# A decode kernel over a 65,536-row cache: V's loads moved from SP's DMA queue to ACT's

## The chip, the core and the metric

The kernel runs on one core of a Trainium2 chip, as one program. The core has a matrix engine (TensorE, PE), a vector engine (VectorE, DVE), a scalar engine (ScalarE, ACT), GpSimd (POOL) and SyncE (SP), each with its own program, and 16 DMA engines that all of them can give transfers to. A transfer is put on the queue of the engine that issues it. The engines wait for each other and for transfers through semaphores that the program names. The metric is the time of one execution on the device in microseconds (us); smaller is better. The median before the change is 2522.78 us over three runs (2522.70 to 2523.16).

## The reference

One token is decoded by an attention block and by a gated MLP, and the two are mixed by a gate:

```python
q = (x @ wq).reshape(B, Sq, H, Dh).transpose(0, 2, 1, 3)          # 1 x 32 x 1 x 128
scores = jnp.einsum("bhqd,bhkd->bhqk", q, k_cache) * (Dh ** -0.5) # k_cache: 1 x 32 x 65536 x 128, bf16
p = softmax(scores, axis=-1)
o = jnp.einsum("bhqk,bhkd->bhqd", p, v_cache)                     # v_cache: as k_cache
a = o.transpose(0, 2, 1, 3).reshape(B, Sq, H * Dh) @ wo
b = (silu(x @ w_gate) * (x @ w_up)) @ w_down                      # 512 -> 1792 -> 512
g = sigmoid((x * gate_w).sum(-1, keepdims=True))
out = g * a + (1 - g) * b
```

The two caches are 32 heads x 65,536 rows x 128 bf16 each, 537 MB each. Each byte is needed once, for one query.

## The kernel before

**Pieces and places.** A head's K and its V are each loaded in two halves of 8.39 MB: 128 partitions with 64 KB each (256 cache rows of 256 bytes), by one DMA. I call them K(h,0), K(h,1), V(h,0) and V(h,1). All lie in one SBUF tensor, `mem`, addressed in KB of a partition (`at(kb, n)`, L107). K(h,0) is at KA = 32 to 96 and K(h,1) at KZ = 0 to 64, so the two overlap in 32 to 64. V(h,0) is at VA = 120 to 184 and V(h,1) at VZ = 96 to 160, overlapping in 120 to 160. A half can therefore be loaded while the other half of its kind is still partly unused, but only when the overlapping part has been used up.

**One head on the engines.** The loop on PE (L486) makes, in iteration i, the scores of head i and the output of head i-1, in this order: scores of K(i,0); a small transposition `turn` (L481); the product with V(i-1,0), 64 matmuls (L501); scores of K(i,1); the product with V(i-1,1), 64 matmuls. DVE transposes each half of K in eight pieces into the double buffer `kt` (L400 for the first half, L407 for the second), and each piece adds 1 to `ktdone`. PE adds 1 to `pvdone` after 40 of the 64 matmuls of a V half (the overlapping part is then used up) and 1 after the last, so 4 for a head. Between heads DVE takes the maximum (L346), POOL spreads it, ACT makes the exponentials (L302), and DVE shuffles them for the V products (L341). ACT also scales the rows of the head before (`row_norm`, L290 to L296).

**SP's queue.** All large loads are issued by SP, in the order of its program: the weights `wq`, `w_gate`, `w_up`, `w_down` and K of head 0 (L211 to L220), then for each h from 1: K(h,0), V(h-1,0), K(h,1), V(h-1,1) (L221 to L233), each after a wait for the count that says that its place is free. At the end come `wo` (L235) and V of head 31, which goes in seven pieces, `tail` (L59, L238 to L245), with a 128 KB piece of `wo` among them. ACT issues three transfers of 1 KB: `x` and `gate_w` at the start (L279, L280) and the output (L311).

**ACT's program.** For each h it waits for the maximum (L299), makes a bias and the exponentials of head h, copies the next query (L305), and then does `row_norm(h - 1)`, which waits for the last V product of that head (L292).

**The end.** After the loop PE does, in this order: `turn` for the last head, `piece(0)` of the tail V, the product with `wo` (L527), `piece(1)`, four small products (L533), and `piece(2)` to `piece(6)`; a last small product and a copy make the output. `piece(n)` waits for the n-th transfer of the tail (L509).

Of the kernel before, what the change touches and what calls it, by code (L numbers as in the profile page):

```python
# [20 lines left out]
def bass_gated_mix__mha_block_cached__swiglu_ffn__decode_kernel(  # L21
# [11 lines left out]
    out: bass.AP,  # L33
):
    _, H, S, Dh = A_k_cache.shape
    D = A_wq.shape[0]
    F = B_w_gate.shape[1]
# [3 lines left out]
    HR = R // 2  # L41
    NP = HR // PR
# [5 lines left out]
    KA, KZ, VA, VZ, V0 = 32, 0, 120, 96, 96  # L48
# [14 lines left out]
    with ExitStack() as ctx:  # L63
# [6 lines left out]
        def sem(name):  # L70
            return ctx.enter_context(nc.semaphore(name))
# [35 lines left out]
        def at(kb, n):  # L107
            return mem[:, kb * KB:kb * KB + n]
# [9 lines left out]
        d = {n: sem("d_" + n) for n in names}  # L118
# [25 lines left out]
        s_b = sem("s_b")  # L144
        s_dch = sem("s_dch")
        ktdone = sem("ktdone")
        qkdone = sem("qkdone")
        pvdone = sem("pvdone")
# [42 lines left out]
        def place(kind, h, z):  # L191
            if kind == "k":
                return (KA, V0)[z] if h == 0 else (KA, KZ)[z]
            return (VA, VZ)[z]

        def kv_dram(cache, h):
            return cache[0, h].rearrange("(b p r) d -> b p (r d)", b=2, p=P)
# [2 lines left out]

        @block.sync
        def _(sp):
            def load(kind, h, z):
                cache = A_k_cache if kind == "k" else A_v_cache
                sp.dma_start(at(place(kind, h, z), HR * Dh), kv_dram(cache, h)[z]).then_inc(d[kind + "az"[z]], 16)

            def weights(n, kb):
                src = w_dram[n]
                sp.dma_start(at(kb, src.shape[1]), src).then_inc(d[n], 16)

            weights("wq", WQ)  # L211
            weights("wg", WG)
            weights("wu", WU)
            weights("wd", WD)
            half = HR // 2 * Dh
            for n in range(2):
                sp.dma_start(at(KA + 32 * n, half), kv_dram(A_k_cache, 0)[0][:, n * half:n * half + half]).then_inc(
                    (d["ka0"], d["ka"])[n], 16)
            sp.wait_ge(s_q, 1)
            load("k", 0, 1)  # L220
            for h in range(1, H):  # L221
                sp.wait_ge(ktdone, 2 * NP * h - 3 if h > 1 else NP)
                load("k", h, 0)
                if h == 1:
                    sp.wait_ge(ktdone, 2 * NP - 3)
                    sp.wait_ge(s_b, 1)
                else:
                    sp.wait_ge(pvdone, 4 * h - 1)
                load("v", h - 1, 0)
                sp.wait_ge(ktdone, 2 * NP * h + NP // 2)  # L230
                load("k", h, 1)
                sp.wait_ge(pvdone, 4 * h + 1)
                load("v", h - 1, 1)  # L233
            sp.wait_ge(ktdone, 2 * NP * H - NP)
            weights("wo", WO)  # L235
            src = A_v_cache[0, H - 1].rearrange("(b p r) d -> b p (r d)", b=2, p=P)
            need = {0: (ktdone, 2 * NP * H - 3), 1: (ktdone, 2 * NP * H), 2: (pvdone, 4 * H - 1)}
            for n, (kb, r0, nr) in enumerate(tail):  # L238
                if n in need:
                    sp.wait_ge(*need[n])  # L240
                b, o = divmod(r0, HR)
                sp.dma_start(at(kb, nr * Dh), src[b][:, o * Dh:(o + nr) * Dh]).then_inc(dt_[n], 16)
                if n == len(tail) - 3:
                    sp.wait_ge(pvdone, 4 * H)
                    sp.dma_start(at(WO31, D), w31_dram).then_inc(d["w31"], 16)  # L245
# [31 lines left out]
        @block.scalar  # L277
        def _(act):
            act.dma_start(xrow[0:1, :], xr_dram).then_inc(d["x"], 16)  # L279
            act.dma_start(gwrow[0:1, :], gw_dram).then_inc(d["gw"], 16)  # L280
            act.wait_ge(s_z, 1)
            nc.scalar.activation(sc[0:1, 1:2], sc[0:1, 0:1], ACT.Exp, scale=-1.0).then_inc(s_e1, 1)
            act.wait_ge(s_qd, 1)
            nc.scalar.copy(qcur[:], qd[:, 0, :, :]).then_inc(s_qc, 1)
            act.wait_ge(s_gp, 1)
            nc.scalar.copy(gcol[:], psM[:, 8:10]).then_inc(s_gc, 1)
            act.wait_ge(s_h, 1)
            nc.scalar.activation(hbuf[:, 0, 0:FC], psM[:, 64:64 + FC], ACT.Exp, scale=-1.0).then_inc(s_sig, 1)

            def row_norm(h):  # L290
                act.wait_ge(s_li, h + 1)
                act.wait_ge(pvdone, 4 * h + 8)  # L292
                act.wait_ge(s_pt, h + 1)
                nc.scalar.mul(orow[0:4, :], psO[0:4, :], Li[0:4, :]).then_inc(s_or, 1)  # L294
                act.wait_ge(s_pt, h + 2)
                nc.scalar.mul(oTn[:, h:h + 1], psT[:, 0:1], gcol[:, 0:1]).then_inc(s_otn, 1)  # L296

            for h in range(H):
                act.wait_ge(s_ar, h + 1)  # L299
                nc.scalar.mul(nbias, amx, -SCALE).then_inc(s_nb, 1)  # L300
                act.wait_ge(s_nb, h + 1)
                nc.scalar.activation(pa[:], psS[:], ACT.Exp, bias=nbias, scale=SCALE,  # L302
                                     accum_out=rsum).then_inc(expdone, 1)
                if h < H - 1:
                    nc.scalar.copy(qcur[:], qd[:, h + 1, :, :]).then_inc(s_qc, 1)  # L305
                if h >= 1:
                    row_norm(h - 1)
            act.wait_ge(s_z4, 1)
            nc.scalar.copy(fin[0:4, :], psZ[0:4, 0:128]).then_inc(s_fin, 1)
            act.wait_ge(s_fin, 1)  # L310
            act.dma_start(out_dram, fin[0:4, :]).then_inc(s_out, 16)  # L311
            act.wait_ge(s_out, 16)
# [261 lines left out]
```

## Time and profile before

| what | value |
|---|---|
| median of three runs | 2522.78 us |
| the profiled execution's own time | 2522.47 us |
| its span, first to last instruction | 2520.7 us |
| busy: PE, DVE, ACT, POOL | 64%, 55%, 3%, 1% of the span |
| HBM read | 1087.77 MB, 432 GB/s over the span |
| granted TensorE clock, mean | 0.702 |

The profile is of one execution. The rows by line name the engine, the operation, what it writes and reads, the count, the busy time and the mean time of one, and then how long the engine stood idle just before and what ended that. In the timeline a row has its start, its length, the engine, the line and, in brackets, the idle time before it. Rows of SPq and ACTq are issues of transfers, not the transfers themselves.

### The profile page before, as it was taken

What the parts mean: (1) busy time and instruction counts of PE and PEld (TensorE: products, weight loads), DVE (VectorE), ACT (ScalarE), POOL (GpSimd) and SP (SyncE); (2) the same over time, 40 slices, a digit from 0 to 9 for tenths busy, and PEclk for the clock granted to TensorE, in tenths of its full rate; (3) what the DMA queues carried; (4) which work ended last, traced back from release to release, by engine and by line L of the source; (5) the groups of instructions that cost most, each with busy time, mean ns of one, the idle gap of its engine ahead of it and who ended that gap; (6) DMA issues with size and microseconds to landing.
All of it is one profiled execution on the core that took longest, in us unless ns stands there. A gap on an engine that the chain in (4) does not pass through costs nothing.

```text
span 2520.7 us, 46415 instructions
## 1 busy us (share of the span) xinstructions
PE 1613.7 (64%) x21429; PEld 920.7 (37%) x21429; DVE 1398.0 (55%) x1629; ACT 65.6 (3%) x195; POOL 27.0 (1%) x83
## 2 busy tenths in 40 slices
PE   4566757656666566566675665666756657657667
PEld 3333333333333333333333333343333333333334
DVE  3765564654655645546556556465464564654653
ACT  0000000000000000000000000000000000000000
POOL 0000000000000000000000000000000000000000
PEclk8567767677677677776776767767767767677677
DMA  9999999999999999999999999999999999999999
GB/s 419 419 433 433 433 433 435 438 438 433 434 433 433 433 434 433 434 433 434 433 433 433 433 433 433 434 437 437 433 435 434 433 433 433 433 434 433 434 433 388
DMA packets 20188, 1088.00 MB, mean 432 GB/s; under 512 B 2250, under 2 KB 2380, under 8 KB 2636
## 3 DMA queue, kind: packets, MB, share of 16 engines
q1 hardware_dynamic: 20160, 1087.78, 99.8%
q8 instruction: 11, 0.18, 0.0%
q14 instruction: 5, 0.04, 0.0%
q10 hardware_dynamic: 12, 0.00, 0.0%
HBM read 1087.77 MB, written 0.00 MB: 432 GB/s over the span
## 4 chain that ended last, share of the span: by engine, by line
DMA 73%; DVE 14%; issue 11%; PE 1%; DVEq 0%; ACT 0%; SPq 0%; POOL 0%
DMA mem<-in_A_k_cache_dram 70%; DVE kt L407 7%; DVE kt L400 6%; DMA mem<-in_A_v_cache_dram 2%; PE psO L501 1%; DVE kt L332 1%; DMA mem<-in_A_wq_dram 1%; PE psM L437 0%; DVE pb L341 0%; DVEq L405 0%; PE psS L453 0%; PE psT L481 0%; DVEq L398 0%; ACT pa L302 0%; DVE sm L346 0%
## 5 line engine op out<-in xcount | busy, mean ns | idle before, releaser
L453 PE MATMUL psS<-qcur,kt 128*128 128x4 bf16 x16384 | 518.7, 167 | 856.9 <-DVE kt L400 438.1
L501 PE MATMUL psO<-mem,pb 128*4 128x512 bf16 x3968 | 998.2, 419 | 18.8 <-DMA mem<-in_A_v_cache_dram 18.8
L407 DVE STREAM_TRANSPOSE kt<-mem 128x2048 uint32<-128x2048 uint32 x248 | 547.6, 2275 | 520.1 <-DMA mem<-in_A_k_cache_dram 520.1
L453 PEld LDWEIGHTS psS<-qcur,kt 128*128 128x128 bf16 x16384 | 476.2, 104 | 925.8 <-DVE kt L400 471.3
L400 DVE STREAM_TRANSPOSE kt<-mem 128x2048 uint32<-128x2048 uint32 x248 | 547.5, 2274 | 417.3 <-DMA mem<-in_A_k_cache_dram 417.2
L501 PEld LDWEIGHTS psO<-mem,pb 128*4 128x4 bf16 x3968 | 357.8, 91 | 631.0 <-issue 191.1
L341 DVE COPY pb<-pa 32x64 bf16<-32x64 bf16 x1024 | 235.2, 230 | 74.6 <-ACT pa L302 51.5
L481 PE MATMUL psT<-unit,orow 4*128 4x1 f32 x256 | 58.8, 347 | 0.8 <-ACT orow L294 0.8
L481 PEld LDWEIGHTS psT<-unit,orow 4*128 4x128 f32 x256 | 56.1, 319 | 1.8 <-ACT orow L294 1.3
L332 DVE STREAM_TRANSPOSE kt<-mem 128x2048 uint32<-128x2048 uint32 x16 | 35.4, 2277 | 16.9 <-DMA mem<-in_A_k_cache_dram 16.9
L346 DVE TENSOR_REDUCE sm<-psS 128x1 f32<-128x512 f32 x32 | 22.1, 692 | 35.5 <-PE psS L453 35.5
L300 ACT ACTIVATE sm<-sm 128x1 f32<-128x1 f32 x32 | 6.5, 203 | 1244.1 <-POOL sm L273 1244.1
L273 POOL PARTITION_ALL_REDUCE sm<-sm x32 | 11.3, 353 | 2393.6 <-DVE sm L346 2393.6
L294 ACT ACTIVATE orow<-psO,sm 4x512 f32<-4x512 f32 x31 | 21.0, 678 | 449.2 <-issue 449.2
L296 ACT ACTIVATE oTn<-psT,gcol 128x1 bf16<-128x1 f32 x31 | 8.2, 264 | 697.7 <-PE psT L481 697.7
L302 ACT ACTIVATE pa<-psS,sm 128x512 bf16<-128x512 f32 x32 | 22.0, 687 | 1.0
L513 PE MATMUL psW<-pb,mem 128*128 128x1 bf16 x512 | 14.4, 165 | 7.8 <-DMA mem<-in_A_v_cache_dram 6.6
L513 PEld LDWEIGHTS psW<-pb,mem 128*128 128x128 bf16 x512 | 13.9, 101 | 8.9 <-issue 7.4
L275 POOL PARTITION_ALL_REDUCE sm<-sm x32 | 12.3, 385 | 36.4 <-ACT pa L302 36.4
L437 PE MATMUL psM<-xTb,mem 128*128 128x1 bf16 x128 | 3.6, 165 | 11.3 <-DMA mem<-in_A_wq_dram 11.3
L465 PE MATMUL psM<-xTb,mem 128*128 128x1 bf16 x112 | 6.9, 198 | 4.8 <-DMA mem<-in_B_w_up_dram 4.8
L423 DVE TENSOR_SCALAR w<-psW,sm 128x4 bf16<-128x4 f32 x1 | 0.2, 228 | 16.9 <-PE psW L513 16.9
(62 smaller groups left out, 65.2 us busy)
## 6 DMA issues: line engine op xcount, KB each, us to landing
mem<-in_A_v_cache_dram SPq DMA_DIRECT2D x3, 4096.0 KB, 28.5
mem<-in_A_k_cache_dram SPq DMA_DIRECT2D x2, 4096.0 KB, 39.0
mem<-in_A_wq_dram SPq DMA_DIRECT2D x1, 4096.0 KB, 12.9
mem<-in_A_wo_dram SPq DMA_DIRECT2D x1, 4096.0 KB, 36.4
mem<-in_A_v_cache_dram SPq DMA_DIRECT2D x1, 2048.0 KB, 33.0
mem<-in_B_w_gate_dram SPq DMA_DIRECT2D x1, 1792.0 KB, 16.7
mem<-in_B_w_up_dram SPq DMA_DIRECT2D x1, 1792.0 KB, 21.4
mem<-in_B_w_down_dram SPq DMA_DIRECT2D x1, 1792.0 KB, 25.2
```

Of the source, the lines that this page charges most:

```text
L275: nc.gpsimd.partition_all_reduce(Lt, rsum, P, RADD).then_inc(s_L, 1)
L294: nc.scalar.mul(orow[0:4, :], psO[0:4, :], Li[0:4, :]).then_inc(s_or, 1)
L302: nc.scalar.activation(pa[:], psS[:], ACT.Exp, bias=nbias, scale=SCALE, accum_out=rsum).then_inc(expdone, 1)
L332: nc.vector.transpose(kt[:, i % 2, :].rearrange("p (j r t) -> p r j t", j=2, t=32), src.rearrange("p (r j t) -> p r j t", j=2, t=32)).then ...
L341: last = nc.vector.tensor_copy(dst, sr)
L346: nc.vector.reduce_max(mxs, psS[:], AX_X).then_inc(s_mx, 1)
L400: nc.vector.transpose(kt[:, c % 2, :].rearrange("p (j r t) -> p r j t", j=2, t=32), src.rearrange("p (r j t) -> p r j t", j=2, t=32)).then ...
L407: nc.vector.transpose(kt[:, c % 2, :].rearrange("p (j r t) -> p r j t", j=2, t=32), src.rearrange("p (r j t) -> p r j t", j=2, t=32)).then ...
L453: last = nc.tensor.matmul(psS[:, col + 4 * r:col + 4 * r + 4], ktb[c % 2][:, je // 2, r, :, je % 2], qcur[:, je, :], start=(je == 0), stop ...
L481: last = nc.tensor.matmul(psT[:, 0:1], orow[0:4, i * Dh:(i + 1) * Dh], unit[0:4, i:i + 1], start=(i == 0), stop=(i == 3))
L501: last = nc.tensor.matmul(psO[0:4, :], pb[:, 256 * z + r:256 * z + r + 4], vt[:, r * Dh:(r + 4) * Dh], start=(z == 0 and part == 0 and m = ...
L513: last = nc.tensor.matmul(psW[:, 0:1], vt[:, r * Dh:(r + 1) * Dh], pb[:, col:col + 1], start=(col == 0), stop=(col == R - 1))
```

## The change

V's loads of heads 0 to 30 leave SP's program and are issued by ACT, on ACT's queue. Their waits are the same counts as before. In ACT's program V(h-1,1) stands at the top of iteration h, ahead of the wait for the maximum, and V(h,0) stands after the copy of the next query and ahead of `row_norm(h - 1)`. V(0,0) stands at the top of iteration 0. SP keeps K, the weights, `wo` and V of head 31, each with its own wait.

```diff
         @block.sync
         def _(sp):
-            def load(kind, h, z):
-                cache = A_k_cache if kind == "k" else A_v_cache
-                sp.dma_start(at(place(kind, h, z), HR * Dh), kv_dram(cache, h)[z]).then_inc(d[kind + "az"[z]], 16)
+            def load(h, z):
+                sp.dma_start(at(place("k", h, z), HR * Dh), kv_dram(A_k_cache, h)[z]).then_inc(d["k" + "az"[z]], 16)
...
-            load("k", 0, 1)
+            load(0, 1)
             for h in range(1, H):
                 sp.wait_ge(ktdone, 2 * NP * h - 3 if h > 1 else NP)
-                load("k", h, 0)
-                if h == 1:
-                    sp.wait_ge(ktdone, 2 * NP - 3)
-                    sp.wait_ge(s_b, 1)
-                else:
-                    sp.wait_ge(pvdone, 4 * h - 1)
-                load("v", h - 1, 0)
+                load(h, 0)
                 sp.wait_ge(ktdone, 2 * NP * h + NP // 2)
-                load("k", h, 1)
-                sp.wait_ge(pvdone, 4 * h + 1)
-                load("v", h - 1, 1)
+                load(h, 1)
             sp.wait_ge(ktdone, 2 * NP * H - NP)
             weights("wo", WO)
...
+            def load(h, z):
+                act.dma_start(at((VA, VZ)[z], HR * Dh), kv_dram(A_v_cache, h)[z]).then_inc(d["v" + "az"[z]], 16)
+
             for h in range(H):
+                if h == 0:
+                    act.wait_ge(ktdone, 2 * NP - 3)
+                    act.wait_ge(s_b, 1)
+                    load(0, 0)
+                else:
+                    act.wait_ge(pvdone, 4 * h + 1)
+                    load(h - 1, 1)
                 act.wait_ge(s_ar, h + 1)
...
                 if h < H - 1:
                     nc.scalar.copy(qcur[:], qd[:, h + 1, :, :]).then_inc(s_qc, 1)
+                if 1 <= h < H - 1:
+                    act.wait_ge(pvdone, 4 * h + 3)
+                    load(h, 0)
                 if h >= 1:
                     row_norm(h - 1)
```

## The prediction

> **What bounds the kernel now.** I read the page first (busy shares, slices, queues, the chain), then the timeline of two heads in the middle, then its start and end.
>
> ```profile
> span 2520.7 us, 46415 instructions
> PE 1613.7 (64%) x21429; PEld 920.7 (37%) x21429; DVE 1398.0 (55%) x1629; ACT 65.6 (3%) x195; POOL 27.0 (1%) x83
> ...
> DMA  9999999999999999999999999999999999999999
> GB/s 419 419 433 433 433 433 435 438 438 433 434 433 433 433 434 433 434 433 434 433 433 433 433 433 433 434 437 437 433 435 434 433 433 433 433 434 433 434 433 388
> ...
> q1 hardware_dynamic: 20160, 1087.78, 99.8%
> ...
> DMA 73%; DVE 14%; issue 11%; PE 1%; DVEq 0%; ACT 0%; SPq 0%; POOL 0%
> ```
>
> No compute engine is above 64%. Every slice has the DMA engines at 9, SP's queue (q1) alone fills 99.8% of their time, and the rate is flat at 433 GB/s. Transfers set the time, and only two things can change it: a moment when no transfer is there, or a longer time for one packet. In the first sense at most 0.2% of 2520.7 us, 5 us, is left to win.
>
> How close SP is to running dry is in the timeline of one head:
>
> ```profile
> 1047.82 0.33 SPq L205 DMA_DIRECT2D mem<-in_A_v_cache_dram  x1
> 1055.13 17.66 DVE L407 STREAM_TRANSPOSE kt<-mem 128x2048 uint32<-128x2048 uint32 x8 [16.96 <-DMA mem<-in_A_k_cache_dram]
> ...
> 1066.24 0.33 SPq L205 DMA_DIRECT2D mem<-in_A_k_cache_dram  x1
> ...
> 1074.41 16.04 PE L501 MATMUL psO<-mem,pb 128*4 128x512 bf16 x64 [0.55 <-DMA mem<-in_A_v_cache_dram]
> ...
> 1085.30 0.33 SPq L205 DMA_DIRECT2D mem<-in_A_v_cache_dram  x1
> ...
> 1093.95 17.66 DVE L400 STREAM_TRANSPOSE kt<-mem 128x2048 uint32<-128x2048 uint32 x8 [13.85 <-DMA mem<-in_A_k_cache_dram]
> ...
> 1102.87 0.33 SPq L205 DMA_DIRECT2D mem<-in_A_k_cache_dram  x1
> ...
> 1132.54 17.66 DVE L407 STREAM_TRANSPOSE kt<-mem 128x2048 uint32<-128x2048 uint32 x8 [16.95 <-DMA mem<-in_A_k_cache_dram]
> ```
>
> K(h,1) to K(h+1,1) takes 1132.54 - 1055.13 = 77.41 us for four halves, 19.35 each; a half gives each of 16 engines eight rows of 64 KB, so a row takes 2.42 us. A half is issued while the one before is still moving. Issue against that one's landing: V(h-1,1) is 7.3 us ahead (1047.82, 1055.13), K(h+1,0) 8.2 (1066.24, 1074.41), V(h,0) 8.65 (1085.30, 1093.95), and K(h+1,1) 10.4 (1102.87; the landing is 1093.95 + 19.35 = 1113.3). These margins are what the change plays with.
>
> **The change, part by part.** *SP loses 62 V issues with their waits.* A K load stood behind a V wait, but never late for it: K(h+1,0) went out at 1066.24, 18.4 us after the V issue ahead of it, and K(h+1,1) 17.6 us after its own. Each was released by its own count of transposes. So K is issued no earlier in the middle: 0 us won.
>
> *ACT gains 62 issues of 0.33 us*, 20.5 us on an engine busy for 65.6. Behind the wait for V(h-1,1) stands the bias of head h. It needs the scores of K(h,1), which PE makes after that V product: the count is there at 1047.82, the bias runs at 1075.07, 27 us later. Behind the wait for V(h,0) stands `row_norm`, whose own wait for the last V product ends at 1090.54, against 1085.30. So ACT delays nothing and issues V at the same moments as SP did; if that cover were gone it would cost 0.33 us an issue. V(0,0) too keeps its moment (77.26; ACT's next work is at 86.17). 0 us.
>
> *Two queues share the engines*, and this is the unknown. Until now the half in flight had the engines alone until it landed; now the next one, issued 7 to 10 us early, competes with it. The nearest row is the only place where both queues carry work, the start: ACT's 1 KB `gate_w` beside SP's `wq`, whose rows are 32 KB, half of 2.42, so 1.21 us.
>
> ```profile
> 1.30 0.23 ACTq L280 DMA_DIRECT2D mem<-in_gate_w_dram  x1
> ...
> 8.09 0.68 DVE L366 CUSTOM_DVE_ANT_0 mem<-mem 1x512 f32<-1x512 bf16 x1 [6.09 <-DMA mem<-in_gate_w_dram]
> ```
>
> It lands 6.8 us after its issue. The queue view puts its data packet into 6.2 to 6.5 us and its last packet into 7.4 to 7.7, one row apart; between 1.3 and 6.3 us SP's queue began 60 packets on 16 engines, 3.75 on each. So one row was moving, about two more went first, and from then on the queues took turns row by row. An idle start costs about 1 us from issue to data (V(0,1) was issued at 122.65 to queues that had just run dry; the share of DMA dips in 122 to 126 alone).
>
> With that rule, K(h+1,0) arrives 1 us after its issue, when V has 7.2 us or 3.0 rows left. One is moving and two are ahead in line, so none to one row of K comes between: V lands at most 2.4 us later. For the 10.4 us margin (3.9 rows) it is one to two rows, up to 4.8 us, of which PE hides 1.2, since it reached that V half 1.2 us after the landing (1036.99 against about 1035.8). The next V issue is late by as much, so the smallest margin falls from 7.3 to between 3.7 and 6 us, still above the 1 us of launch. No engine runs dry: 0 us. The other end of this cost: equal shares from the moment of arrival, 0.6 to 1.9 us a head (rival B), 18 to 57 us in 30 heads. I take 0, since the only row with both queues shows whole rows and a line ahead.
>
> [...]
>
> *The end.* SP used to issue `wo` behind the last V wait; the row order shows it.
>
> ```profile
> 2440.98 0.33 SPq L205 DMA_DIRECT2D mem<-in_A_v_cache_dram  x1
> 2441.35 0.43 SPq L209 DMA_DIRECT2D mem<-in_A_wo_dram  x1
> ...
> 2468.09 15.53 PE L501 MATMUL psO<-mem,pb 128*4 128x512 bf16 x64 [0.55 <-DMA mem<-in_A_v_cache_dram]
> ...
> 2484.43 1.05 PE L481 MATMUL psT<-unit,orow 4*128 4x1 f32 x8 [0.82 <-ACT orow L294]
> ...
> 2487.61 3.51 PE L513 MATMUL psW<-pb,mem 128*128 128x1 bf16 x128 [2.13 <-DMA mem<-in_A_v_cache_dram]
> ...
> 2507.06 3.55 PE L513 MATMUL psW<-pb,mem 128*128 128x1 bf16 x128 [2.48 <-DMA mem<-in_A_v_cache_dram]
> ```
>
> Now `wo` waits only for head 31's first eight transposes (done at about 2428) and stands behind K(31,1), ahead of or beside V(30,1), issued at 2441. Eight rows of `wo` (4.19 MB, 9.7 us) go in among V's eight, so V(30,1) lands up to 9.7 us later: PE starts it at 2477.8, ends at 2493.3, `turn` ends at 2495.2 instead of 2485.5. `piece(0)` used to wait 2.13 us for its data, so it starts at 2495.2, 7.6 late. The work up to `piece(2)` is PE's own chain (its 2.48 us wait is the only slack): `piece(2)` begins at 2504.6 + 7.7 = 2512.3, ends at 2515.85, then 112 matmuls at 27.7 ns (3.1) and the last 16 (0.44) end at 2519.4, against 2517.86 before, where the last rows wait for data. The end moves by 1.5 us. Bounds: 0, if V goes first, and 7.2, if all of the 9.7 counts but the 2.48.
>
> **Sum.** 0 + 0 + 0 + 1.5 on the profiled 2522.47 us (span 2520.7 and 1.8 around it), which stands 0.3 below the median: 2522.78 + 1.5 = 2524.3, rounded up to 2524.4 for what is rounded off above.
>
> **The rivals.**
>
> B, slower: *the queues run dry once a head.* It is one mechanism: K(h+1,1) takes half of the rate as soon as it arrives. V(h,0) has 9.4 us left, lands 9.4 us later, at 1045.2 in the numbers of the head above, so PE starts it 8.2 us late and V(h,1) goes out at 1056.0, data at 1057.0; K landed at 1055.1. Dry for 1.9 us, in each head until K's own delay gives V a start: V(h+1,0) then begins 1.2 us ahead, and the next gap is 0.7. With 1.0 us a head, 30 heads give 30 us: 2553 (2541 to 2580). It decides from a delay of V(h,0) above 1.2 + 7.3 - 1.0 = 7.5 us, three rows. For it: with nothing in line ahead, 3.9 rows are already that many. Against it: `gate_w`'s row.
>
> C, slower: *the tail takes the whole delay of V(30,1)*, 7.2 us, as when `wo` and the tail pieces overtake and the DVE and ACT steps between are late as well: 2530. Against it: the 2.13 and 2.48 us waits in the rows.
>
> D, slower: *a packet costs more beside another queue's*. With 0.5% on 2480 us of halves, 12 us: 2535. For it: nothing in this profile, as only `gate_w`'s two packets stand among another queue's.
>
> E, faster: *two queues close the last gaps.* All of the 0.2% idle share, 5 us, and 438 in place of 433 GB/s in some slices: 2517 at best. Against it: no slice below 433 but the first two and the last.
>
> **How the numbers follow.** The forecast 0.54, B 0.26, C 0.09, D 0.07, E 0.04. The measurement tells about 0.2%, 5 us, from no change. The forecast is the same within that, E counts 0.03 as faster and 0.01 as same; B, C and D are slower: 0.03, 0.55, 0.42. The range runs from 2520, below the forecast's end bound of 0, to 2553, the middle of B, which leaves out half of B and most of E, some 0.17. The forecast's own range is 2521 to 2528.
>
> **What would show it.** Right: in the changed profile two queues of about 520 MB (ACT's) and 568 MB (SP's), shares that add up to 99% or more, 77.4 us from K(h,1) to K(h+1,1), V's issue 3 to 7 us ahead of the landing before it, PE's first wait for V(h,0) 1 to 4 us longer, `piece(2)` without a wait. Wrong: a period of 78 us or more with slices below 433 GB/s (B if the DMA share dips once a head, D if it does not), or a tail longer by more than 5 us (C).

## The result and the profile after

The changed kernel takes 2591.14 us (median of four runs, 2581.24 to 2601.63) against 2522.74 before: ratio 1.0272, 95% interval 1.0256 to 1.0288. It is slower by 68 us, where no change was forecast. Its runs also spread over 20 us, where those of before lie within 1. The profiled execution took 2585.45 us, with a span of 2583.6 against 2520.7: 62.9 us to explain.

The page of the changed kernel, by engine, slice, queue and chain, and its costliest group:

```profile
span 2583.6 us, 46415 instructions
...
DMA  9999999999999999999999999999999999999998
GB/s 419 428 425 431 412 391 436 408 390 406 437 423 435 408 403 425 423 435 425 422 422 431 429 425 435 422 438 435 409 406 422 434 426 422 438 422 422 427 433 361
...
q1 hardware_dynamic: 11232, 567.68, 50.8%
q10 hardware_dynamic: 8940, 520.10, 47.4%
...
DMA 71%; PE 27%; DVE 2%; issue 0%; ACT 0%; POOL 0%; DVEq 0%
...
L505 PE MATMUL psO<-mem,pb 128*4 128x512 bf16 x3968 | 986.1, 415 | 366.4 <-DMA mem<-in_A_v_cache_dram 366.4
```

The bytes are the same, now on two queues (q10 is ACT's); in every kernel here only SP and ACT issue transfers, so no run shows the queue of another engine. The two queues' shares add up to 98.2%, where one queue had 99.8%, and the flat 433 GB/s has become 390 to 438, without the last slice. The tenths of the DMA row are too coarse to show it. PE waited 18.8 us in all for V before; now it waits 366.4 us. The chain of waits ran over K's transfers and DVE (70% and 14% of the span); it now runs over V's and PE's product with them (68% and 26%), since the release of the next V comes last. The row of the product in the kernel before:

```profile
L501 PE MATMUL psO<-mem,pb 128*4 128x512 bf16 x3968 | 998.2, 419 | 18.8 <-DMA mem<-in_A_v_cache_dram 18.8
```

The timeline of a head of the changed kernel, from the landing of K(h,1) to the next (issues, the transposes of K, PE's products with V):

```profile
1009.46 0.33 ACTq L290 DMA_DIRECT2D mem<-in_A_v_cache_dram  x1
1010.80 4.50 DVE L411 STREAM_TRANSPOSE kt<-mem 128x2048 uint32<-128x2048 uint32 x2 [17.00 <-DMA mem<-in_A_k_cache_dram]
...
1036.28 15.91 PE L505 MATMUL psO<-mem,pb 128*4 128x512 bf16 x64 [6.41 <-DMA mem<-in_A_v_cache_dram]
...
1047.04 0.33 ACTq L290 DMA_DIRECT2D mem<-in_A_v_cache_dram  x1
1050.98 17.67 DVE L404 STREAM_TRANSPOSE kt<-mem 128x2048 uint32<-128x2048 uint32 x8 [14.87 <-DMA mem<-in_A_k_cache_dram]
...
1077.41 14.96 PE L505 MATMUL psO<-mem,pb 128*4 128x512 bf16 x60 [5.89 <-DMA mem<-in_A_v_cache_dram]
...
1088.09 0.34 ACTq L290 DMA_DIRECT2D mem<-in_A_v_cache_dram  x1
1089.57 4.50 DVE L411 STREAM_TRANSPOSE kt<-mem 128x2048 uint32<-128x2048 uint32 x2 [16.95 <-DMA mem<-in_A_k_cache_dram]
```

PE stands still for about 6 us before each V half; before it was 0.55 us and nothing. So V is issued late: V(h,0) 3.9 us ahead of K's landing (1047.04 to 1050.98), where it was 8.65, and V(h,1) 1.5 us ahead (1088.09 to 1089.57), where it was 7.3. K's own last rows end at 1088.46 to 1089.06, before its landing is seen, and the first row of this V half starts at 1089.07, 0.98 us after its issue, so the engines run dry. The stretches of the trace show the moment (the last two columns are the DMA share, booked where a packet starts, and the rate):

```profile
1086.00:1088.00 2.00, 2.00 (x11) 0.80 (x10) 0.00 (x0) 0.00 (x0) 0.00 (x0) 1.00 1.21 524
1088.00:1089.00 1.00, 1.00 (x7) 0.37 (x5) 0.00 (x0) 0.00 (x0) 0.00 (x0) 1.00 0.01 0
1089.00:1090.00 1.00, 1.00 (x6) 0.40 (x5) 0.43 (x1) 0.00 (x0) 0.00 (x0) 1.00 3.08 1049
```

No row of data starts from 1088 to 1089. The head takes 1089.57 - 1010.80 = 78.77 us instead of 77.41, 1.36 lost. Other heads lose up to 6 (83.43 us from 526.40 to 609.83): between 516 and 600 us PE waits 9 to 10 us before each V half, and single engines are dry for over 4 us at a time there.

Why V lands late is in the records of single packets, which the trace keeps for each transfer (strung together to 16 engines by their starts and ends). On one engine the rows went, K for SP's queue, V for ACT's, with the increment of the semaphore marked *:

```
V1050.1 V1052.5 V1054.9 V1057.3 V1059.7 V1062.1 K1064.6 V1067.0 K1069.4 V1071.8 K1074.2 V*1076.6 K1076.6
```

K(h+1,1) was issued at 1059.90. The row then moving and one more of V went first; from then on the queues took turns. Two rows of K came between V's last three rows, and a third before V's *increment*: 7.3 us in all. The increment is a packet of its own, and it too waits its turn. In the half before, the count is one row and one more, 4.8 us. Over the whole run 99% of V's 992 increments start more than 1 us after their last row, the median 2.411 us, one row of K; in the kernel before none of SP's 2240 does. The queue view shows the increments alone, for the 1 us in which those of V(h-1,1) were written (1035.2 to 1036.2): 15 packets of 4 bytes, beside 15 rows of K that begin there.

```profile
q1 hardware_dynamic: 15, 0.98, 226.7%
q10 hardware_dynamic: 15, 0.00, 0.8%
```

The same records give an account of the lost time. "Dry" is the mean time over 16 engines in which an engine moved nothing; "longer rows" is what rows took beyond 2.418 us for 64 KB. Both are differences to the kernel before (8.7 and 6.1 us). Nearly all of the changed kernel's longer rows, 23.3 of 28.0 us ahead of this subtraction, are first rows behind a gap or behind the other queue's last increment, not rows inside the alternation.

| kernel (profiled run) | span less 2520.7 | dry | longer rows |
|---|---|---|---|
| changed kernel | 62.9 | 41.0 | 22.0 |
| K(h,1) later | 25.6 | 15.0 | 10.8 |
| V in two waits | 27.5 | 10.1 | 18.9 |
| only V(h,0) on ACT | 75.0 | 44.3 | 30.8 |
| only V(h,1) on ACT | 25.6 | 8.4 | 17.3 |
| V in 32 KB rows | 497.4 | 461.9 | 36.6 |

The other kernels are experiments of the next section. The two columns add up to the loss within 2 us in every kernel; since all move the same bytes, they nearly must, so they say where the time lies and not why.

The end of the changed kernel, from the landing of K(31,1), for a reading further below:

```profile
2506.34 17.73 DVE L411 STREAM_TRANSPOSE kt<-mem 128x2048 uint32<-128x2048 uint32 x8 [16.97 <-DMA mem<-in_A_k_cache_dram]
...
2537.75 16.10 PE L505 MATMUL psO<-mem,pb 128*4 128x512 bf16 x64 [12.61 <-DMA mem<-in_A_v_cache_dram]
...
2573.60 3.55 PE L517 MATMUL psW<-pb,mem 128*128 128x1 bf16 x128 [0.86 <-issue]
```

And the same landing in the kernel before:

```profile
2448.80 17.66 DVE L407 STREAM_TRANSPOSE kt<-mem 128x2048 uint32<-128x2048 uint32 x8 [16.95 <-DMA mem<-in_A_k_cache_dram]
```

### The profile page after: what moved, and what is told of

Read it like the earlier page. It is cut to its first block, busy times and chain, and to the rows that moved or that the text cites. A ratio compares the mean times of both kernels' runs of the same rounds, so it can differ in the third digit from the quotient of the medians.

```text
span 2583.6 us, 46415 instructions
## 1 busy us (share of the span) xinstructions
PE 1592.2 (62%) x21429; PEld 909.8 (35%) x21429; DVE 1400.2 (54%) x1629; ACT 65.6 (3%) x195; POOL 27.0 (1%) x83
## 4 chain that ended last, share of the span: by engine, by line
DMA 71%; PE 27%; DVE 2%; issue 0%; ACT 0%; POOL 0%; DVEq 0%
DMA mem<-in_A_v_cache_dram 68%; PE psO L505 26%; DMA mem<-in_A_k_cache_dram 2%; DVE kt L336 1%; DMA mem<-in_A_wq_dram 0%; DVE kt L404 0%; PE psW L517 0%; PE psY L531 0%; DVE pb L345 0%; PE psM L441 0%; PE psS L457 0%; PE psT L485 0%; PE psZ L537 0%; DVE amat L419 0%; ACT pa L303 0%
## 5 line engine op out<-in xcount | busy, mean ns | idle before, releaser
L505 PE MATMUL psO<-mem,pb 128*4 128x512 bf16 x3968 | 986.1, 415 | 366.4 <-DMA mem<-in_A_v_cache_dram 366.4
L457 PE MATMUL psS<-qcur,kt 128*128 128x4 bf16 x16384 | 510.2, 166 | 600.2 <-DVE kt L404 319.2
L457 PEld LDWEIGHTS psS<-qcur,kt 128*128 128x128 bf16 x16384 | 468.1, 102 | 666.6 <-DVE kt L404 350.0
L531 PE MATMUL psY<-mem,oR 128*1 128x512 bf16 x32 | 8.5, 434 | 0.3 <-DVE oR L422 0.3
## 6 DMA issues: line engine op xcount, KB each, us to landing
mem<-in_A_v_cache_dram SPq DMA_DIRECT2D x3, 4096.0 KB, 27.5
```

Source lines behind the costliest of these rows:

```text
L457: last = nc.tensor.matmul(psS[:, col + 4 * r:col + 4 * r + 4], ktb[c % 2][:, je // 2, r, :, je % 2], qcur[:, je, :], start=(je == 0), stop ...
L505: last = nc.tensor.matmul(psO[0:4, :], pb[:, 256 * z + r:256 * z + r + 4], vt[:, r * Dh:(r + 4) * Dh], start=(z == 0 and part == 0 and m = ...
```

## The experiments

The theory after the result: the two queues take turns packet by packet, so the half in flight pays one row of the other queue for each of its last rows and one more for its increment; the next V is released late by that, and the engines run dry. Rival 1: ACT as issuer, or its queue, is slow. Rival 2: two streams cost rate wherever they lie beside each other. Rival 3 came up later: each half that is moved costs a share of its own.

**One queue, ACT's.** The loads of the head loop all go to ACT, in the order that SP had.

```diff
             for h in range(1, H):
-                sp.wait_ge(ktdone, 2 * NP * h - 3 if h > 1 else NP)
-                load(h, 0)
-                sp.wait_ge(ktdone, 2 * NP * h + NP // 2)
-                load(h, 1)
+                if h == 1:
+                    sp.wait_ge(ktdone, NP)
+                    load(1, 0)
...
                 nc.scalar.mul(orow[0:4, :], psO[0:4, :], Li[0:4, :]).then_inc(s_or, 1)
+                if h + 2 < H:
+                    act.wait_ge(ktdone, 2 * NP * (h + 2) + NP // 2)
+                    loadk(h + 2, 1)
...
                     load(h - 1, 1)
+                    if h < H - 1:
+                        act.wait_ge(ktdone, 2 * NP * (h + 1) - 3)
+                        loadk(h + 1, 0)
...
```

> All loads of K and V in the head loop are issued by ACT on its own queue, in the order that SP had before (K(1,0) and the first loads stay with SP). Theory (turns between two queues: the last rows of a V half and its increment each wait for a row of K on the other queue, so V lands 5 to 7 us late, the next V is issued late, and the engines run dry once a head): with one queue there are no turns, 2520 to 2526 us, and K(h,1) to K(h+1,1) 77.4 us. Rival 1 (ACT as issuer, or its queue, is the slow thing; V's transfers are the ones with longer rows): 2560 us or more. Rival 2 (two streams read side by side cost rate wherever they overlap): 2520 to 2526 too.

Measured: 2527.96 us, ratio 1.0021 (1.0011 to 1.0030). Its queues and the timeline of a head:

```profile
q10 hardware_dynamic: 17724, 1031.81, 94.4%
q1 hardware_dynamic: 2448, 55.97, 5.2%
```

```profile
1047.86 0.34 ACTq L292 DMA_DIRECT2D mem<-in_A_v_cache_dram  x1
1054.89 17.67 DVE L422 STREAM_TRANSPOSE kt<-mem 128x2048 uint32<-128x2048 uint32 x8 [16.96 <-DMA mem<-in_A_k_cache_dram]
...
1066.00 0.33 ACTq L295 DMA_DIRECT2D mem<-in_A_k_cache_dram  x1
...
1074.17 16.31 PE L516 MATMUL psO<-mem,pb 128*4 128x512 bf16 x64 [0.55 <-DMA mem<-in_A_v_cache_dram]
```

V is 7.0 us ahead again, PE waits 0.55 us, and from 150 us to 2440 us an engine is dry for 0.08 us at the mean, as before the change. Rival 1 falls for the heads: ACT can issue the heads' loads and its queue can carry them (1031.81 MB) at the old pace. But 5 us are left, more than the theory gave.

**K(h,1) one transpose later**, with two queues:

```diff
-                sp.wait_ge(ktdone, 2 * NP * h + NP // 2)
+                sp.wait_ge(ktdone, 2 * NP * h + NP // 2 + 1)
```

> The changed kernel, with SP's wait for K(h,1) raised by one transpose (2.2 us). Two queues as in the changed kernel. Theory (turns): K arrives one row later, so two rows of K instead of three go between V(h-1,0)'s rows and its increment; V lands 2.4 us earlier and the next V is issued before K has run out: 2522 to 2540 us, and PE's wait for V before the first product of a head falls from 5.9 to about 3.5 us. Rivals 1 and 2 (ACT's queue slow; overlap costs rate): no change, 2575 us or more.

Measured: 2557.1 us (2548.12 to 2579.08), ratio 1.0164 (1.0115 to 1.0214). At the median the loss is halved, which neither rival allows, though one of the four runs lies where they put it (2575 or more); and the median lies 17 us above what the theory gave. PE's wait before the first product of a head fell as expected, from 5.89 to 3.62 in this head, and the one before the second from 6.41 to 0.57:

```profile
1047.26 15.57 PE L505 MATMUL psO<-mem,pb 128*4 128x512 bf16 x64 [3.62 <-DMA mem<-in_A_v_cache_dram]
...
1083.58 8.62 PE L505 MATMUL psO<-mem,pb 128*4 128x512 bf16 x29 [0.57 <-DMA mem<-in_A_v_cache_dram]
```

What it does not cure is K's own increments, which the theory had left out: 45% of the 1248 on SP's queue now wait for a row of V, where 7% did. The loss of the profiled run is 15.0 us of dry time, half of it between 2000 and 2440 us, and 10.8 us of longer rows.

**V in 32 KB rows**, two DMAs for a half, K as before:

```diff
-                act.dma_start(at((VA, VZ)[z], HR * Dh), kv_dram(A_v_cache, h)[z]).then_inc(d["v" + "az"[z]], 16)
+                n = HR // 2 * Dh
+                for i in range(2):
+                    act.dma_start(at((VA, VZ)[z] + 32 * i, n),
+                                  kv_dram(A_v_cache, h)[z][:, n * i:n * i + n]).then_inc(d["v" + "az"[z]], 16)
...
-                        pe.wait_ge(d["v" + "az"[z]], i * 16)
+                        pe.wait_ge(d["v" + "az"[z]], i * 32)
```

> The changed kernel, with each V half in two DMAs of 32 KB rows (PE waits for both). K keeps 64 KB rows. Theory (turns, one packet each whatever its size): beside K, V gets a third of the rate instead of half, and has 16 rows and two increments that each wait for a K row: above 2700 us. Rivals 1 and 2: the same bytes beside each other, 2575 to 2610 us.

Measured, one run: 3019.91 us. The page of this kernel:

```profile
DMA  9979878797897887978888788887978888889898
```

The same bytes, in packets of half the size on one of the two queues, cost 497 us, almost all of it dry time. This is the strongest of the runs: under a share by bytes the size of a packet would not count. In the records of the changed kernel a turn is one row; with that, V beside K gets half of K's bytes (an estimate from rows of 32 and 64 KB). PE waits 885.7 us in all for V here, where the changed kernel has 366.4. Rival 2 falls as the main cause. The packet records say the same: in the changed kernel a row that follows one of the other queue without a gap is longer by 10 ns (V behind K, 1390 rows) or 1 ns (K behind V, 2267 rows).

**V in two waits.** Each V half goes in the 5/8 that PE uses first and the rest, with a semaphore each, and PE waits for the second only before its last 24 matmuls.

```diff
...
-                act.dma_start(at((VA, VZ)[z], HR * Dh), kv_dram(A_v_cache, h)[z]).then_inc(d["v" + "az"[z]], 16)
+                cuts = ((0, HR - V_KEEP), (HR - V_KEEP, HR)) if z == 0 else ((V_KEEP, HR), (0, V_KEEP))
+                for (r0, r1), s in zip(cuts, (d["v" + "az"[z]], d["v" + "az"[z] + "2"])):
+                    act.dma_start(at((VA, VZ)[z] + r0 // 4, (r1 - r0) * Dh),
+                                  kv_dram(A_v_cache, h)[z][:, r0 * Dh:r1 * Dh]).then_inc(s, 16)
...
                         for part, rows in enumerate(v_order[z]):
+                            if part == 1:
+                                pe.wait_ge(d["v" + "az"[z] + "2"], i * 16)
```

> The changed kernel, with each V half in two DMAs with a semaphore each: the 5/8 that PE uses first (40 KB rows) and the rest (24 KB rows). PE's first 40 matmuls wait for the first part alone, so that the count that releases the next V comes earlier by some 5 us. Two queues as before, with more turns. Theory (what costs is that V is released late, so the engines run dry): 2520 to 2530 us. Rivals 1 and 2 (ACT's queue slow; overlap costs rate): 2575 us or more.

Measured: 2546.87 us, ratio 1.0091 (1.0074 to 1.0108). Two thirds of the loss are gone although there are more turns than ever, so it is the late release that costs. The last third stayed, against the expectation: K now takes more turns beside the shorter rows (42% of the increments on SP's queue wait), and 19 us are longer rows.

**Half of the move.** Only V(h,0) on ACT, and only V(h,1) on ACT; the other half stays on SP's queue at its old place.

```diff
                 load(h, 1)
+                sp.wait_ge(pvdone, 4 * h + 1)
+                sp.dma_start(at(VZ, HR * Dh), kv_dram(A_v_cache, h - 1)[1]).then_inc(d["vz"], 16)
...
-                else:
-                    act.wait_ge(pvdone, 4 * h + 1)
-                    load(h - 1, 1)
```

And the other kernel, with V(h,0) back between SP's K loads:

```diff
                 load(h, 0)
+                if h == 1:
+                    sp.wait_ge(ktdone, 2 * NP - 3)
+                    sp.wait_ge(s_b, 1)
+                else:
+                    sp.wait_ge(pvdone, 4 * h - 1)
+                sp.dma_start(at(VA, HR * Dh), kv_dram(A_v_cache, h - 1)[0]).then_inc(d["va"], 16)
...
-                if 1 <= h < H - 1:
-                    act.wait_ge(pvdone, 4 * h + 3)
-                    load(h, 0)
```

> Only the first half of each V, V(h,0), is issued by ACT; V(h,1) is back on SP's queue behind K(h+1,1). Theory (turns; the loss is a release that comes after the queues have run dry, not the turns themselves): V(h,0) starts ahead of K(h+1,0)'s landing again, since V(h-1,1) is no longer late, and the three rows of K then leave a margin: 2523 to 2540 us, well under half of the changed kernel's loss. Rival 3 (each moved half costs its share, the losses add): some 30 to 45 us, 2553 to 2568, and the losses of this kernel and of the one that moves only V(h,1) add to the changed kernel's 60 to 70.

> Only the second half of each V, V(h,1), is issued by ACT; V(h,0) is back on SP's queue between K(h+1,0) and K(h+1,1). Theory (turns): one row of K and one more before the increment, V 4.8 us late in that half alone; the next K and V(h,0) stand in order on SP's queue, so nothing runs dry: 2523 to 2535 us. Rival 3 (losses add): 25 to 40 us, 2548 to 2563.

Measured: V(h,0) alone 2581.63 us, ratio 1.0235 (1.0219 to 1.0250); V(h,1) alone 2550.89, ratio 1.0117 (1.0101 to 1.0132). My expectations fell for both: 59 and 28 us. Rival 3 is no better. Its ranges hold the second and not the first, and the two add to 87, more than the whole change costs. One engine's rows with V(h,0) on ACT (K stands for all of SP's queue) show where I had gone wrong:

```
K1036.7 V1039.2 K1041.6 V1044.0 K*1046.4 V1046.4 V1048.8 ... V1058.5 K1060.9 V*1063.3 K1063.3
```

I had counted the turns that V pays. With V(h,0) issued early again, it is K(h+1,0) that pays, two rows, and K's transposes, the next K and all that stands behind it on SP's queue go late: PE waits 618.6 us in all for the transposes of K's first halves, where it was 438.1 before the change, and 69.8 for V. So here K was the late one, and in the changed kernel V: of two halves on two queues the one that was ahead was delayed, in the heads shown by 4.8 us here (two rows) and by 4.8 and 7.3 there. Why the one kernel loses twice as much as the other was not tried.

**wo behind V(30,1)**, on top of one queue for the head loop, for the 5 us left there:

```diff
             sp.wait_ge(ktdone, 2 * NP * H - NP)
+            sp.wait_ge(pvdone, 4 * H - 3)
             weights("wo", WO)
```

> The kernel with all loads of the head loop on ACT's queue, and SP's load of wo held back until the count that releases V(30,1), as it stood before the change. Theory (what is left there of 5 us is wo going ahead of V(30,1), so that PE's closing chain starts late): 2522 to 2524 us, and the idle time of PE before piece(2) is back at about 2.5 us. Rival (ACT as issuer costs 5 us): 2527 to 2529.

Measured: 2528.34 us, ratio 1.0021 (1.0012 to 1.0030). Nothing won, and the timeline of its end says why:

```profile
2442.33 0.36 ACTq L293 DMA_DIRECT2D mem<-in_A_v_cache_dram  x1
2442.39 0.33 SPq L208 DMA_DIRECT2D mem<-in_A_wo_dram  x1
...
2480.32 15.83 PE L517 MATMUL psO<-mem,pb 128*4 128x512 bf16 x64 [10.26 <-DMA mem<-in_A_v_cache_dram]
```

V(30,1) and `wo` are issued in the old order, 0.06 us apart, but here, on two queues, the order of issue did not keep V ahead: PE waits 10.26 us for V where it waited 0.55, which is what eight turns with rows of `wo` would add (8 x 1.21 = 9.7 us, an estimate from the rows of `wq`). That left ACT as issuer open, so the next kernel takes `wo` and the tail to ACT's queue as well.

**One queue for all.** SP keeps only the loads up to K(1,0).

```diff
...
+                    else:
+                        act.dma_start(at(WO, w_dram["wo"].shape[1]), w_dram["wo"]).then_inc(d["wo"], 16)
+                        for n in range(2):
+                            act.wait_ge(ktdone, 2 * NP * H - 3 * (1 - n))
+                            tail_load(n)
...
```

> As the kernel with all loads of the head loop on ACT's queue, with wo and the tail of V moved to ACT's queue too, in the order before the change; SP keeps only the loads up to K(1,0). Theory (the last 5 us are wo and the tail taking turns with V(30,1), which goes on whatever their order of issue while they stand on another queue): 2522 to 2524 us, V(30,1) again no more than 1 us late for PE. Rival (ACT as issuer costs 5 us): 2527 to 2529.

Measured: 2523.27 us against 2522.67, ratio 1.0002 (0.9993 to 1.0011). In the timeline of its end PE waits for V(30,1) as before the change, and `piece(2)` waits for its data again:

```profile
2469.59 15.44 PE L523 MATMUL psO<-mem,pb 128*4 128x512 bf16 x64 [0.55 <-DMA mem<-in_A_v_cache_dram]
...
2508.52 3.55 PE L535 MATMUL psW<-pb,mem 128*128 128x1 bf16 x128 [2.52 <-DMA mem<-in_A_v_cache_dram]
```

So the issuer costs nothing that can be measured, and the 5 us were `wo` and the tail on a second queue, the same step that costs the changed kernel 5.4 us at its end. The second queue costs everything.

**K in 32 KB rows**, V with 64 KB rows, two queues:

```diff
+                n = HR // 2 * Dh
+                for i in range(1 if h == 0 else 2):
+                    m = HR * Dh if h == 0 else n
+                    sp.dma_start(at(place("k", h, z) + 32 * i, m),
+                                 kv_dram(A_k_cache, h)[z][:, m * i:m * i + m]).then_inc(d["k" + "az"[z]], 16)
...
-                dma = i * 16
+                dma = i * 32
```

> The changed kernel, with each K half from K(1,0) on in two DMAs of 32 KB rows; V keeps 64 KB rows. Theory (one packet a turn): V waits less at each turn (1.2 us), but beside V K gets a third of the rate and has 16 rows and two increments that each wait for a V row of 2.4 us, so K becomes the late one: 2600 to 2680 us. Rivals 1 and 2 (ACT's queue slow; overlap costs rate): 2575 to 2605.

Measured, one run: 2570.29 us, a miss: below the changed kernel, not above. V's increments now wait 1.206 us at the median, half of 2.411 and one row of K, as the turns say. But K did not become as late as I had it: PE waits 506.3 us in all for the transposes of K's first halves, where it was 438.1 before the change, and 110.1 for V, where the changed kernel has 366.4. I had let K and V overlap for a whole half; they overlap only at the end of one. With a single run beside a spread of 20 us, no more is read from it.

**Both K halves one transpose later:**

```diff
-                sp.wait_ge(ktdone, 2 * NP * h - 3 if h > 1 else NP)
+                sp.wait_ge(ktdone, 2 * NP * h - 2 if h > 1 else NP)
...
-                sp.wait_ge(ktdone, 2 * NP * h + NP // 2)
+                sp.wait_ge(ktdone, 2 * NP * h + NP // 2 + 1)
```

> The changed kernel, with SP's waits for both K halves raised by one transpose (2.2 us). Theory (turns): fewer rows of K go ahead of V's increments in both halves, so V is released before K has run out: below the 2557 us of the kernel that raises only K(h,1)'s wait, 2523 to 2550. If K is released too late by it, so that K is what runs dry: above 2557. Rivals 1 and 2: 2575 or more.

Measured: 2574.7 us (2561.76 to 2585.92), ratio 1.0222 (1.0190 to 1.0254), with the median above 2557: the second branch, though the runs of the two kernels overlap. V's increments that wait are down from 99% to 51%, but 41% of those on SP's queue wait now, and K's first rows behind V's increments are longer by 11.7 us in all, where it was 0.3. Holding K back moves the loss from V to K: PE waits 88.1 us in all for V, where the changed kernel has 366.4, and 473.6 for the transposes of K's first halves, where it has 319.2.

**The gap at 122 us**, in the kernel before: V(0,1) in two DMAs, the 24 KB whose place is free early right behind K(1,1).

```diff
+                if h == 1:
+                    keep = V_KEEP * Dh
+                    sp.dma_start(at(VZ, keep), kv_dram(A_v_cache, 0)[1][:, 0:keep]).then_inc(d["vz"], 16)
+                    sp.wait_ge(pvdone, 4 * h + 1)
+                    sp.dma_start(at(VA, HR * Dh - keep), kv_dram(A_v_cache, 0)[1][:, keep:]).then_inc(d["vz"], 16)
...
-                        pe.wait_ge(d["v" + "az"[z]], i * 16)
+                        pe.wait_ge(d["v" + "az"[z]], i * 16 + 16 * z)
```

> The kernel before, one queue on SP, with V(0,1) in two DMAs: its last 24 KB of each partition, whose place is free early, goes right behind K(1,1), the other 40 KB when V's count releases them. Theory (the only time before the end at which the engines run dry is 122 to 125 us, where V(0,1) is released 1 us before K(1,1) is through: 1.6 us dry and 0.7 us of longer first rows): 2520 to 2521.5 us, 1 to 2.5 us faster than before. Rival (that gap is hidden by later work): 2522.5 to 2523.

Measured: 2521.52 us (11 runs, 2521.18 to 2521.80) against 2522.64 (21 runs, 2521.68 to 2524.44), ratio 0.9996, interval 0.9987 to 1.0005. The records show 1.0 us less dry time in the first 150 us. It is the lowest median of all, but the interval holds 1, so it is not shown to be faster.

## Why the prediction was wrong, step by step

- *What bounds the kernel* held: transfers set the time, and a second queue could win nothing. *SP's V waits delayed no K* and *ACT delays nothing* hold too: with all loads on ACT the time is that of before.
- *Two queues share the engines* is the step that failed, at "V lands at most 2.4 us later". The turns by rows were right, read from `gate_w`'s two packets. But that row had also shown the last packet of a transfer, its increment, standing one row apart from the data, and the sum counted data rows only. One more row of K goes before each increment. Also, one more row of V and not two went ahead of K, so the rows came out at the upper ends. Measured in the head above: 4.8 us instead of 0 to 2.4, and 7.3 us instead of up to 4.8.
- With 7.3 us the delay stands just below the point from which rival B was said to decide (7.5 us), and the smallest margin fell to 1.5 us, not to between 3.7 and 6. The limit itself, 1 us of launch, was too low: it was set against the landing that DVE sees, at 1089.57, but K's last increments start at 1088.5 to 1089.1, so 1.5 us of margin was not enough. So rival B came: dry once a head. Its price was mis-sized, 30 us against 57.5 in the profiled run up to K(31,1)'s landing (2506.34 - 2448.80). It had no term for the first rows behind a gap or another queue's end (most of the 22 us of longer rows), and in some heads single engines were dry for over 4 us. B's way of sharing, equal parts from arrival, was wrong; turns reach the same delay.
- "The only row with both queues" was one transfer of 1 KB, and the prediction let it decide between 0 and 57 us. The margin of 7.3 us was known, the delay known only to a row or two, and these were the same size: that was a case for B at even odds, not 0.26.
- *The end* was right in its mechanism: V(30,1) lands late behind `wo`, and `piece(2)` no longer waits for data. Its size was not: from K(31,1)'s landing to the end it is 77.3 us (2583.6 - 2506.34) against 71.9 (2520.7 - 2448.80), 5.4 more where the step said 1.5; by the prediction's own sign, a tail longer by more than 5 us, rival C came as well. PE waits 12.61 us for V(30,1): the 0.55 of before, the 9.7 forecast and one more row for the increment. That row accounts for 2.4 of the 3.9 us that the step missed; the rest was not traced.
- *Rival D*, a packet that costs more beside another queue's (its 0.5% was assumed, not read from a row), is refuted for rows inside the alternation by the 10 and 1 ns. It holds for the first row of V behind K's last increment without a gap: 0.16 us longer at the mean (558 rows), 5.6 us in all. *Rival E* had nothing to win.

What stays open: why some heads lose 1.4 us and others 6, and why executions of the same program differ by 20 us. The order of the turns differs from head to head in the records; what sets it was not tried.

## What to carry to other kernels

Here transfers filled the time (99.8% of the engines' time in the kernel before), and the order on one queue was worth keeping: with the loads in that order on SP's queue the kernel took 2522.67 us, on ACT's (all but the first loads) 2523.27, with V on a second queue 2591.14. Before splitting loads over two queues, set the smallest lead of an issue over the landing ahead of it against one packet of the other queue for each packet left and one more for the increment. Here that was 7.3 us against three rows of 2.42, 7.3 us; the two were of one size, and the engines ran dry for 41.0 us more than before. The size of the packets counted too: V in 32 KB rows beside K's 64 KB took 3019.91 us, K in 32 KB rows beside V's 64 KB 2570.29 (one run each), both in 64 KB rows 2591.14. V was the half that PE waited for (366.4 us in all with 64 KB rows), and shorter rows for it made that 885.7 us.

## What the runs showed of the hardware that was not expected

- The increment of a transfer takes a turn of its own: V's start 2.411 us (median) behind the last row beside K's 64 KB rows, in the changed kernel, and 1.206 us beside 32 KB rows, in the kernel with K in 32 KB rows.
- In the changed kernel turning from one queue to the other costs next to nothing while both are at work (10 ns and 1 ns). There a first row behind a gap is longer by 0.66 us at the mean (396 rows of V behind K's increment).
